# One row of w, one more transpose by DMA, products moved to GpSimd, and a new order for 889 tasks

## The chip, the cores and the metric

The kernel runs on one core of a Trainium2 chip. That core has five engines with queues of their own: TensorE (PE in the profile; its weight loads are PEld), VectorE (DVE), ScalarE (ACT), GpSimd (POOL) and SyncE (SP), and 16 DMA engines that all queues share. The metric is the device time of one execution in microseconds (us); lower is better. The kernel before takes 161.94 us (median of three runs, 161.53 to 162.7).

## The reference

Two layers follow each other. The first is a linear attention with a decaying state, for 4 batches, 8 heads, 768 steps and 48 channels a head:

```python
for t in range(S):
    kt, vt, rt = (k[:, :, t], v[:, :, t], r[:, :, t])
    cur = np.einsum('bhd,bhe->bhde', u[None] * kt, vt)
    y[:, :, t] = np.einsum('bhd,bhde->bhe', rt, state + cur)
    state = w[None, :, :, None] * state + np.einsum('bhd,bhe->bhde', kt, vt)
```

Its output, with the heads side by side, is x (4 batches of 768 x 384). The second is an MLP mixer, first over the tokens, then over the channels:

```python
xt = x.transpose(0, 2, 1)
h = np.maximum(xt @ w_tok1, 0.0) @ w_tok2
u = x + h.transpose(0, 2, 1)
h2 = np.maximum(u @ w_ch1, 0.0) @ w_ch2
return u + h2
```

w_tok1 is 768 x 256, w_ch1 is 384 x 1536. All inputs and the output are float32; the kernel multiplies in bfloat16.

## The kernel before, in words

**Tiling.** Batches are numbered b=0 to 3 in the code. A batch has six chunks of 128 steps. Within a chunk the attention is done with matrices: k and r are scaled by powers of w (tables that ScalarE makes once, as the exponential of ln w times a position), turned so that the channels lie on the partitions, and multiplied into scores (`sc`, tile at_ps). A mask cuts the scores (tile AT, on VectorE), and `y` takes AT times v plus r times the state S of the chunks before. What a step adds with its own k and v (the part with the vector u of the input) is a sum over r, k and u (tile adg) times v (`own`, tiles yd and ydb). The result is x_b, in bfloat16.

b=0 takes its chunks in three pairs (`pair_unit`): one load brings two chunks, the four scaled products of a pair (`scaled`, k and r, two each) multiply two operands in SBUF, PE turns them, and wide copies of 1024 columns (`evac_k`, `evac_r`) bring them out of PSUM. b=1 turns by PE as well; b=2 and b=3 turn k and r by a DMA transpose from SP's queue (`turn_rk`).

**Mixer.** Each batch has: `hid` (tile h_ps, with w_tok1, then a relu to h1r), `back` (with w_tok2), the channel layer `up` (tile z_ps: 24 tasks of three matmuls a batch, twelve for each half `sg` of the tokens), a relu to zr on ScalarE or VectorE, and `down` (tile h_ps, three steps of four products for each of six token blocks), then a sum or copy to osb and a store.

The layer `up` needs u = x + h turned. There are two ways, chosen by the list `DIRECT` for each (batch, half):

- direct: PE turns x (`turn_x`, nine matmuls of 128 columns), adds the backward product on top in the turned form (`back_T`), and three copies out of PSUM give uT. u itself is never made in its plain form; so the last `down` step of each block adds it with three more matmuls of 128 columns (tile h_ps from ident and uT), and the output is a copy.
- not direct: `back` gives h in the plain form, three sums on VectorE make u (`sum_u`, tile u_sb), one DMA transpose on SP's queue makes uT (`turn_dma`), and the output is a sum of u and the `down` product on VectorE.

**Order.** Everything is a task. `ORDER` lists all task numbers, written out by hand; the kernel emits its instructions in that order, so it is the program order of every engine and queue. `ENGINES` says, for each task that can go either way, which of its two engines takes it (for a product of two SBUF operands 0 is GpSimd and 1 VectorE). `BUFS` gives the buffer number of each tile, and with it what a task must wait for before it can overwrite. Twenty tasks of PE (`keep_warm`, tile kv_ps from warm) are matmuls of 512 columns without a use, put between the first real ones.

**Start.** w is read as two rows of 192, to partitions 0 and 64 (`read_w`, lines 355 to 359). Each row is spread to 128 partitions by a matmul with ones (`spread_w`, lines 447 to 451), ScalarE takes ln of each half (line 454), and the tables follow (`decay`, line 467). The weights are read by DMAs from GpSimd's queue (`load_weights`, line 581): the two token weights first, then two parts of w_ch1, then three of w_ch2. In that queue they stand between GpSimd's products.

```python
DIRECT = [(0, 0), (0, 1), (1, 0)]
PRODUCT = {"POOL": "mul2_POOL", "DVE": "mul2_DVE"}
w_rows = [wp[z * P:z * P + 1, 0, 0:dm // 2] for z in range(2)]
```

Nearly all instructions carry line 274 in the profile, which is the helper that records every operation; they are told apart by their tiles.

Of the kernel before, what the change touches and what calls it, by code (L numbers as in the profile page):

```python
# [11 lines left out]
f32 = mybir.dt.float32  # L12
# [54 lines left out]
    0, 1, 2, 0, 1, 0, 2, 0, 1, 2, 0, 1, 2, 1, 0, 1, 2, 1, 0, 2, 1, 0, 2, 1,  # L67
    ],
    'AT1': [
    0, 1, 2, 0, 1, 0, 2, 0, 1, 2, 0, 2, 1, 0, 2, 1, 0, 2, 1, 0, 2, 0, 1, 2,  # L70
# [11 lines left out]
    0, 1, 2, 3, 4, 0, 1, 2, 3, 0, 4, 3, 1, 2, 3, 0, 4, 2,  # L82
# [11 lines left out]
    0, 1, 2, 3, 4, 5, 0, 2, 1, 5, 3, 4, 0, 3, 2, 1, 0, 5, 3, 4, 2, 1, 5, 3, 0, 4, 2,  # L94
# [3 lines left out]
    0, 1, 2, 3, 4, 5, 0, 1, 2, 4, 3, 5, 4, 1, 2, 3, 5, 0,  # L98
# [16 lines left out]
    ],  # L115
    'osb': [
    0, 1, 2, 0, 2, 2, 0, 2, 0, 1, 0, 0, 2, 1, 0, 1, 0, 1, 1, 0, 2, 0, 1, 2, 0,
# [8 lines left out]
    0, 1, 2, 3, 0, 1, 2, 3, 0, 1, 2, 3,  # L126
# [9 lines left out]
    0, 1, 1, 0, 1, 0, 1, 0, 1, 0, 0, 1,  # L136
    ],
    'rt': [
    0, 1, 2, 3, 4, 2, 0, 1, 3, 2, 4, 0,
# [3 lines left out]
    0, 1, 2, 3, 0, 1, 2, 3,  # L143
    ],
    'u_sb': [
    0, 1, 2, 1, 2, 0, 1, 2,
    ],
    'vb': [
    0, 1, 2, 3, 4, 0, 1, 2, 3, 0, 4, 1, 2, 0, 3, 1, 4, 0,
    ],  # L150
    'vt': [
    0, 1, 2, 3, 4, 5, 1, 0, 2, 3, 4, 1, 5, 0, 2, 3, 4, 1,
# [5 lines left out]
    0, 1, 2, 0, 1, 2, 0, 1, 2, 0, 1, 2, 2, 1, 0, 2, 1, 0,  # L158
# [5 lines left out]
    0, 1, 2, 0, 1, 2, 0, 1, 2, 0, 1,  # L164
    ],
}
ENGINES = [
# [21 lines left out]
    0, 1, 2, 3, 4, 5,  # L189
]  # L190
H1_PARTS = [[(0, 1), (2, 3), (4, 5)], [(0, 1, 2, 3, 4, 5)], [(0, 1, 2, 3, 4, 5)], [(0, 1, 2, 3, 4, 5)]]
DIRECT = [(0, 0), (0, 1), (1, 0)]
PART = 4
STORE = ['SP', 'SP', 'SP', 'SP']

# [40 lines left out]
def kernel(  # L236
# [73 lines left out]
    def row(src):  # L310
        return src.rearrange("h d -> (h d)")
# [930 lines left out]
```

## Time and profile before

| | |
|---|---|
| median of three runs | 161.94 us |
| the profiled execution | 161.46 us |
| its span, first to last instruction | 159.8 us |
| TensorE busy | 154.1 us, 1584 matmuls |
| VectorE busy | 116.2 us, 231 instructions |
| ScalarE busy | 74.0 us, 167 |
| GpSimd busy | 71.1 us, 96 |
| DMA | 26.31 MB, 165 GB/s in the mean |
| granted TensorE clock | 0.998 |

The page gives the busy time of each engine, the span in 40 slices of 4 us with the busy share in tenths, and the chain that ended last: from the last instruction back, at each step to what released it. A line of a group reads: engine, operation, output tile <- input tiles, shapes, count | busy us in all, ns of one | idle time of the engine before them, and who ended it. A line of the chain or of a timeline begins with its start and its length in us. For a DMA issue the time is the issue's; the landing has a line of its own.

### The profile page before, as it was taken

How to read it: one execution, taken by the hardware profiler on the slowest of the kernel's cores; microseconds unless marked ns; L12 is line 12 of the kernel's file. 1: busy time of each engine (PE TensorE's matmuls, PEld its weight loads, DVE VectorE, ACT ScalarE, POOL GpSimd, SP SyncE). 2: the span in 40 equal slices, each digit the busy share in tenths (PEclk: the TensorE clock that was granted, in tenths of full speed). 3: DMA queues.
4: the chain of work that ended last, by engine and by line, in shares of the span. 5: the costliest groups of instructions: out<-in, count | busy, mean ns of one | idle time of the engine just before them, and what ended most of it. 6: DMA issues, size and time to landing. Idle time of an engine off the chain costs nothing.

```text
span 159.8 us, 3993 instructions
## 1 busy us (share of the span) xinstructions
PE 154.1 (96%) x1584; PEld 103.5 (65%) x1584; DVE 116.2 (73%) x231; ACT 74.0 (46%) x167; POOL 71.1 (45%) x96
## 2 busy tenths in 40 slices
PE   6999899999999899999999999999999999999992
PEld 2475676767776576667667766677666656666662
DVE  6499997777987589879999839978988363620422
ACT  3784685649977432264722541167431202365000
POOL 7599872392970403559163465419854000000000
PEclk9999999999999999999999999999999999999999
DMA  4999999989799797869999998998990146040052
GB/s 125 264 242 216 187 228 211 206 176 230 125 226 219 136 219 174 181 120 174 213 196 225 247 228 101 220 240 178 151 181 4 49 102 146 8 144 0 3 194 98
DMA packets 86824, 26.31 MB, mean 165 GB/s; under 512 B 81555, under 2 KB 85910, under 8 KB 86806
## 3 DMA queue, kind: packets, MB, share of 16 engines
q1 hardware_dynamic: 81328, 22.22, 68.5%
q0 software_dynamic: 5280, 3.74, 15.5%
q8 instruction: 12, 0.20, 0.5%
q10 hardware_dynamic: 198, 0.11, 0.2%
q14 instruction: 6, 0.05, 0.1%
HBM read 20.46 MB, written 4.72 MB: 158 GB/s over the span
## 4 chain that ended last, share of the span: by engine, by line
PE 84%; DVE 5%; DMA 5%; POOL 1%; issue 1%; ACT 1%; DVEq 0%; ACTq 0%
PE h_ps L274 33%; PE z_ps L274 27%; PE kv_ps L274 6%; DMA wch<-in_moe_w_ch_dram 5%; PE y_ps L274 5%; PE at_ps L274 3%; PE hT_ps L274 3%; PE hx_ps L274 3%; DVE kr L274 2%; PE tr_ps L274 2%; DVE AT L274 1%; PE w_ps L274 1%; POOL kr L274 1%; ACT S L274 1%; DVE zr L274 1%
## 5 line engine op out<-in xcount | busy, mean ns | idle before, releaser
L274 PE MATMUL h_ps<-wch,zr 128*128 128x384 bf16 (+1 forms) x300 | 52.7, 319 | 0.4 <-DMA wch<-in_moe_w_ch_dram 0.4
L274 PE MATMUL z_ps<-uT,wch 128*128 128x384 bf16 x288 | 52.1, 327 | 0.0
L274 ACT ACTIVATE zr<-z_ps 128x384 bf16<-128x384 f32 x62 | 28.2, 494 | 27.9 <-PE z_ps L274 27.2
L274 PEld LDWEIGHTS <-wch 128*128 128x128 bf16 x288 | 30.9, 114 | 12.5 <-DMA uT<-u_sb 0.2
L274 PEld LDWEIGHTS <-zr 128*128 128x128 bf16 x300 | 27.9, 98 | 16.7 <-issue 0.7
L274 DVE TENSOR_SCALAR zr<-z_ps 128x384 bf16<-128x384 f32 x34 | 18.1, 552 | 11.4 <-PE z_ps L274 11.2
L274 DVE TENSOR_TENSOR AT<-at_ps,mask 128x512 bf16<-128x512 f32 x36 | 22.9, 680 | 2.3 <-PE at_ps L274 2.3
L274 POOL TENSOR_TENSOR yd<-vb,adg 128x384 f32<-128x384 bf16 x15 | 12.3, 831 | 25.6 <-ACT vb L274 14.5
L274 DVE TENSOR_TENSOR osb<-u_sb,h_ps 128x384 f32<-128x384 bf16 (+1 forms) x16 | 8.4, 526 | 14.1 <-PE h_ps L274 13.7
L274 PEld LDWEIGHTS <-kr 128*128 128x128 bf16 (+1 forms) x196 | 12.6, 98 | 4.8 <-issue 1.3
L274 ACT CAST S<-kv_ps 48x192 bf16<-48x192 f32 (+1 forms) x26 | 9.1, 351 | 13.9 <-PE kv_ps L274 9.7
L274 POOL TENSOR_TENSOR kr<-rt,wp 128x384 bf16<-128x384 f32 x8 | 9.7, 1221 | 10.6 <-ACT wp L274 8.3
L274 POOL TENSOR_TENSOR kr<-kt,wnat 128x384 bf16<-128x384 f32 x8 | 8.4, 1053 | 7.3 <-ACT wnat L274 3.9
L274 DVE TENSOR_TENSOR x_b<-y_ps,yd 128x384 bf16<-128x384 f32 x18 | 9.8, 551 | 2.6 <-PE y_ps L274 2.2
L274 PEld LDWEIGHTS <-wtok 128*128 128x128 bf16 x78 | 7.3, 98 | 4.5 <-DVE x_b L274 0.2
L274 ACT CAST vb<-vt 128x384 bf16<-128x384 f32 x18 | 9.0, 514 | 2.4 <-DMA vt<-in_v_dram 2.4
L274 PE MATMUL kv_ps<-warm 128*128 128x512 bf16 x20 | 7.6, 505 | 1.4 <-DVE warm L274 1.4
L274 PE MATMUL h_ps<-x_b,wtok 128*128 128x384 bf16 x48 | 8.6, 326 | 0.0
L274 DVE TENSOR_TENSOR u_sb<-x_b,hT_ps 128x384 bf16<-128x384 bf16 x15 | 7.7, 549 | 1.3 <-PE hT_ps L274 1.2
L274 POOL TENSOR_TENSOR ku<-kt,u_bc 128x384 f32<-128x384 f32 x8 | 8.0, 1003 | 1.3 <-DVE rku L274 1.3
L274 DVE TENSOR_TENSOR AT<-at_ps,u_sb 128x512 bf16<-128x512 f32 x12 | 7.9, 680 | 0.3 <-PE at_ps L274 0.2
L274 ACT ACTIVATE h1r<-h_ps 128x384 bf16<-128x384 f32 x5 | 2.3, 490 | 10.4 <-PE h_ps L274 10.4
(104 smaller groups left out, 207.8 us busy)
## 6 DMA issues: line engine op xcount, KB each, us to landing
out_dram<-osb SPq DMA_DIRECT2D x23, 192.0 KB, 2.0
kt<-in_k_dram SPq DMA_DIRECT2D x18, 192.0 KB, 6.0
vt<-in_v_dram SPq DMA_DIRECT2D x18, 192.0 KB, 4.4
rt<-in_r_dram SPq DMA_DIRECT2D x12, 192.0 KB, 3.7
wch<-in_moe_w_ch_dram POOLq DMA_DIRECT2D x4, 384.0 KB, 6.3
zr<-in_r_dram SPq DMA_DIRECT2D x3, 384.0 KB, 4.8
zr<-in_k_dram SPq DMA_DIRECT2D x3, 384.0 KB, 5.5
win<-in_r_dram SPq DMA_DIRECT2D x3, 384.0 KB, 8.1
```

The costliest lines, as they stand in the source:

```text
L274: return lambda *args, **kw: tc.keep_in_program_order(f(*args, **kw))
```

## The change

Four things.

1. w is read as one row of 384 with one DMA, spread by one matmul and taken through one ln.
2. `DIRECT` loses (1, 0): the first half of u of b=1 (the second batch) goes the way that is not direct. So PE's `turn_x` and `back_T` of it become `back`, three copies become three sums on VectorE, one DMA transpose joins SP's queue, the last `down` steps of that half lose their three matmuls, and its three outputs become sums on VectorE.
3. `ENGINES` is anew. Of the twelve scaled products of b=0, GpSimd has four (all of the third pair) and VectorE eight; before it was two and ten. Other choices differ too: of the products of k, r and u of b=2, GpSimd has 17 of 24 and VectorE 7, before 10 and 14.
4. `ORDER` and `BUFS` are anew: 889 tasks instead of 894.

```diff
 ORDER = [
-    2, 26, 14, 19, 25, 0, 886, 24, 59, 10, 63, 62, 884, 9, 878, 888, 3, 16, 4, 1, 5, 22, 28, 60, 66, 29, 6,
...
+    21, 57, 3, 0, 22, 18, 24, 19, 11, 1, 58, 56, 16, 25, 2, 59, 8, 869, 62, 887, 6, 4, 13, 5, 60, 883, 63,
...
 ]
 BUFS = {
...
     'u_sb': [
-    0, 1, 2, 1, 2, 0, 1, 2,
+    0, 1, 2, 1, 2, 0, 2, 1, 0,
     ],
...
 }
 ENGINES = [
-    0, 1, 1, 1, 1, 1, 1, 1, 1, 0, 1, 1, 0, 0, 0, 0, 0, 0, 0, 0, 1, 1, 0, 1, 1, 0, 0, 0, 0, 0, 0, 1, 0, 0, 0,
...
+    1, 0, 0, 1, 0, 0, 1, 1, 1, 0, 1, 1, 1, 1, 0, 0, 0, 1, 1, 0, 1, 1, 0, 1, 1, 0, 1, 0, 0, 0, 0, 1, 0, 0, 0,
...
 ]
-DIRECT = [(0, 0), (0, 1), (1, 0)]
+DIRECT = [(0, 0), (0, 1)]
...
-    ones = const.tile([P + 1, 128], f32, name="ones")
+    ones = const.tile([1, 128], f32, name="ones")
...
-    w_rows = [wp[z * P:z * P + 1, 0, 0:dm // 2] for z in range(2)]
+    w_row = wp[0:1, 0, :]
...
-    def read_w(z):
-        return lambda: act.dma_start(w_rows[z], row(w)[z * dm // 2:(z + 1) * dm // 2].unsqueeze(0))
-
-    t_wrow0 = once("ACT", "dma_tiny", read_w(0))
-    t_wrow = once("ACT", "dma_tiny_b", read_w(1), [t_wrow0])
+    t_wrow = once("ACT", "dma_tiny", lambda: act.dma_start(w_row, row(w).unsqueeze(0)))
...
-            pe.matmul(U[key], ones[0:1, :], src, start=True, stop=True)
+            pe.matmul(U[key], ones, src, start=True, stop=True)
...
-    t_wbc = [once("PE", f"spread_{z}", spread_w(z), [(t_wrow0, t_wrow)[z], t_ones], take=("m",)) for z in range(2)]
-    t_lnw = [once("ACT", "act192", ln_w(z), [t_wbc[z], t_tab], use=[(t_wbc[z], "m")]) for z in range(2)]
+    t_wbc = once("PE", "spread", spread("w", w_row), [t_wrow, t_ones], take=("m",))
+    t_lnw = once("ACT", "act384", lambda: act.activation(lnw, U["w"], Ln), [t_wbc, t_tab], use=[(t_wbc, "m")])
...
```

More of the change, by code (lines that the diff above doesn't have):

```diff
@@ L66 @@
     'AT0': [
-    0, 1, 2, 0, 1, 0, 2, 0, 1, 2, 0, 1, 2, 1, 0, 1, 2, 1, 0, 2, 1, 0, 2, 1,
+    0, 1, 2, 0, 2, 0, 1, 0, 2, 1, 0, 1, 2, 0, 1, 2, 0, 1, 2, 0, 1, 2, 0, 2,
     ],
     'AT1': [
-    0, 1, 2, 0, 1, 0, 2, 0, 1, 2, 0, 2, 1, 0, 2, 1, 0, 2, 1, 0, 2, 0, 1, 2,
+    0, 1, 2, 0, 2, 0, 1, 0, 2, 1, 0, 2, 1, 0, 2, 1, 0, 2, 1, 0, 2, 1, 0, 2,
     ],
@@ L81 @@
     'adg': [
-    0, 1, 2, 3, 4, 0, 1, 2, 3, 0, 4, 3, 1, 2, 3, 0, 4, 2,
+    0, 1, 2, 3, 4, 1, 0, 3, 2, 4, 1, 0, 2, 3, 1, 4, 0, 1,
     ],
@@ L93 @@
     'kp': [
-    0, 1, 2, 3, 4, 5, 0, 2, 1, 5, 3, 4, 0, 3, 2, 1, 0, 5, 3, 4, 2, 1, 5, 3, 0, 4, 2,
+    0, 1, 2, 3, 4, 5, 2, 3, 5, 0, 1, 4, 3, 2, 5, 0, 1, 2, 5, 4, 3, 0, 2, 1, 4, 3, 5,
     ],
@@ L97 @@
     'kt': [
-    0, 1, 2, 3, 4, 5, 0, 1, 2, 4, 3, 5, 4, 1, 2, 3, 5, 0,
+    0, 1, 2, 3, 4, 5, 0, 1, 3, 2, 4, 5, 0, 1, 3, 4, 2, 5,
     ],
@@ L106 @@
     'm': [
[8 rows of a table removed]
[8 rows of a table added]
     ],
     'osb': [
-    0, 1, 2, 0, 2, 2, 0, 2, 0, 1, 0, 0, 2, 1, 0, 1, 0, 1, 1, 0, 2, 0, 1, 2, 0,
+    0, 1, 2, 0, 0, 2, 0, 2, 1, 0, 2, 0, 1, 1, 2, 1, 0, 2, 0, 1, 2, 0, 1, 2, 0,
     ],
@@ L125 @@
     'rk': [
-    0, 1, 2, 3, 0, 1, 2, 3, 0, 1, 2, 3,
+    0, 1, 2, 3, 0, 1, 2, 3, 1, 0, 2, 3,
     ],
@@ L135 @@
     'rku': [
-    0, 1, 1, 0, 1, 0, 1, 0, 1, 0, 0, 1,
+    0, 1, 0, 1, 0, 1, 0, 1, 0, 0, 1, 0,
     ],
     'rt': [
-    0, 1, 2, 3, 4, 2, 0, 1, 3, 2, 4, 0,
+    0, 1, 2, 3, 4, 0, 2, 1, 4, 0, 3, 1,
     ],
@@ L142 @@
     'uT': [
-    0, 1, 2, 3, 0, 1, 2, 3,
+    0, 1, 2, 3, 1, 0, 2, 3,
     ],
     'u_sb': [
-    0, 1, 2, 1, 2, 0, 1, 2,
+    0, 1, 2, 1, 2, 0, 2, 1, 0,
     ],
     'vb': [
-    0, 1, 2, 3, 4, 0, 1, 2, 3, 0, 4, 1, 2, 0, 3, 1, 4, 0,
+    0, 1, 2, 3, 4, 1, 0, 3, 2, 4, 1, 0, 3, 2, 4, 1, 0, 2,
     ],
     'vt': [
-    0, 1, 2, 3, 4, 5, 1, 0, 2, 3, 4, 1, 5, 0, 2, 3, 4, 1,
+    0, 1, 2, 3, 4, 5, 1, 0, 2, 3, 4, 5, 1, 2, 0, 3, 4, 5,
     ],
@@ L157 @@
     'yd': [
-    0, 1, 2, 0, 1, 2, 0, 1, 2, 0, 1, 2, 2, 1, 0, 2, 1, 0,
+    0, 1, 2, 1, 0, 2, 1, 0, 2, 1, 0, 2, 0, 1, 2, 1, 0, 2,
     ],
@@ L163 @@
     'zr': [
-    0, 1, 2, 0, 1, 2, 0, 1, 2, 0, 1,
+    0, 1, 2, 2, 0, 1, 0, 2, 1, 0, 2,
     ],
@@ L443, in f @@
             U[key] = ps(f"{key}_ps", [128, dm])
-            pe.matmul(U[key], ones[0:1, :], src, start=True, stop=True)
+            pe.matmul(U[key], ones, src, start=True, stop=True)
         return f
-    def spread_w(z):
-        def f():
-            U["w", z] = ps(f"w{z}_ps", [128, dm // 2])
-            pe.matmul(U["w", z], ones[z * P:z * P + 1, :], w_rows[z], start=True, stop=True)
-        return f
-    def ln_w(z):
-        return lambda: act.activation(lnw[:, z * dm // 2:(z + 1) * dm // 2], U["w", z], Ln)
-    t_wbc = [once("PE", f"spread_{z}", spread_w(z), [(t_wrow0, t_wrow)[z], t_ones], take=("m",)) for z in range(2)]
-    t_lnw = [once("ACT", "act192", ln_w(z), [t_wbc[z], t_tab], use=[(t_wbc[z], "m")]) for z in range(2)]
+    t_wbc = once("PE", "spread", spread("w", w_row), [t_wrow, t_ones], take=("m",))
+    t_lnw = once("ACT", "act384", lambda: act.activation(lnw, U["w"], Ln), [t_wbc, t_tab], use=[(t_wbc, "m")])
     t_wd = once("PE", "tiny_mm", cast_wd, [t_wh, t_idf], take=("m",))
@@ L468, in decay @@
         return once("ACT", "act384s", lambda: act.activation(t[:, g, :], lnw, Exp, scale=iota[:, col:col + 1]),
-                    t_lnw + deps)
+                    [t_lnw] + deps)
     t_wp2 = [decay(wp2, j, 2 + j, [t_io2]) for j in range(2)]
     t_wk2 = [once("ACT", "act384s", lambda j=j: act.activation(early["wk", j], lnw, Exp, scale=iota[:, j:j + 1]),
-                  t_lnw + [t_io2, t_ewk[j]], use=use_wk[j]) for j in range(2)]
+                  [t_lnw, t_io2, t_ewk[j]], use=use_wk[j]) for j in range(2)]
     t_wn = {G: [decay(wn[G], g, (4 if G == 2 else 6) + g, [t_io]) for g in range(G)] for G in USED}
@@ L510 @@
     wps = {3: wp}
-    t_wp = {3: [decay(wp, g, 6 + NG + g, [t_io, t_us, t_wd, t_ud, t_uw] + t_wbc) for g in range(NG)]}
+    t_wp = {3: [decay(wp, g, 6 + NG + g, [t_io, t_wbc, t_us, t_wd, t_ud, t_uw]) for g in range(NG)]}
     if 2 in TABLES:
```

114 rows, old and new, of tables (BUFS, ENGINES, ORDER) are left out of this document.

## The prediction

> **What bounds the kernel now.** I read the busy table first, then the slices of the DMA engines, then the chain of work that ended last, and after that the queues of the engines the change touches.
>
> ```profile
> span 159.8 us, 3993 instructions
> PE 154.1 (96%) x1584; PEld 103.5 (65%) x1584; DVE 116.2 (73%) x231; ACT 74.0 (46%) x167; POOL 71.1 (45%) x96
> DMA  4999999989799797869999998998990146040052
> ```
>
> TensorE (PE) is busy 154.1 of 159.8 us; no other engine comes near. The DMA engines stand at eight or nine tenths in nearly every slice up to the thirtieth (120 us), so they are the second bound: loads must be asked for early, and little is left for more.
>
> The chain in order of time shows where PE was not the one that counted:
>
> ```profile
> 1.39 1.89 PE kv_ps L274 x4
> 3.28 1.59 PE w_ps L274 x4
> ...
> 15.26 2.66 DVE kr L274 x2
> ...
> 28.41 2.30 PE hx_ps L274 x22
> ...
> 44.44 8.20 DMA wch<-in_moe_w_ch_dram
> ...
> 62.72 0.17 PE hx_ps L274 x3
> ...
> 100.62 0.55 PE at_ps L274 x16
> ...
> 105.09 3.90 PE z_ps L274 x24
> ...
> 156.85 0.36 DVE osb L274
> ```
>
> ```profile
> PE h_ps L274 <- DMA wch<-in_moe_w_ch_dram: 0.4, 1, 0.4
> ```
>
> PE works from 1.39 to about 156.85. Of its 5.7 us without work (159.8 - 154.1), 1.39 lie before and 2.95 (159.8 - 156.85) behind, so 1.4 us are all that any new order could still fill. The rest of the chain that is not PE is two VectorE (DVE) products at 15.26, and one weight load that landed at 52.64 (44.44 + 8.20) and for which, by the table of waits, PE stood 0.4 us. A matmul of 384 columns costs 3.90/24 = 162.5 ns, one of 128 columns 0.17/3 = 57 ns; so four of the first take 0.65.
>
> **Time outside the span.** The profiled execution took 161.46 for a span of 159.8, so 1.66 lie around it; the median 161.94 is 0.48 above that execution. I work in the span and add 2.14.
>
> **First u of b=1 by DMA.** Removed from PE: nine turns of x and nine additions of u in the last down steps, all of 128 columns. The `back` products stay six of 384 columns, only with the operands exchanged. PE saves 18 x 57 ns = 1.0 us, on the path, since PE is full there.
>
> ```profile
> L274 ACT CAST uT<-hx_ps 128x384 bf16<-128x384 f32 x5 | 2.3, 482 | 3.7 <-PE hx_ps L274 3.7
> L274 DVE TENSOR_TENSOR u_sb<-x_b,hT_ps 128x384 bf16<-128x384 bf16 x15 | 7.7, 549 | 1.3 <-PE hT_ps L274 1.2
> L274 SPq DMA_TRANSPOSE uT<-u_sb x5: 1249/1292/2010, 68.1 to 132.8; - x5
> DMA to landing us min/median/max: 4.0/4.0/4.0
> ```
>
> Instead of a 0.48 us copy, the first `up` now waits for a DVE sum and a DMA that lands 4.0 us after SyncE (SP) starts to issue it. The u's three chunks leave PE 2 x 162.5 = 325 ns apart and a sum takes 549, so the last sum ends 0.55 + 2 x 0.22 = 1.0 after the last product: 5.0 us to the landing. What covers it: behind the last of these products the new list has seven PE tasks before the first `up`: three `down` (0.65), three `down` that end in a residual (0.65 + 0.17 = 0.82) and one score of two chunks (0.55), 4.96 us. No slack, and just ahead in SP's queue stands the turn of a k and r of b=2, another transpose, whose issue takes as long as this one's, 1.29. I take 0.4 us of new waiting; the ends are 0 and 1.3, more if loads block SP (first rival). The three DVE sums (1.65 us) replace two copies on ACT and one on DVE; of the three outputs of this u, two go from ACT to DVE (1.1). DVE's idle time, below, covers both.
>
> **w as one row.** One DMA, one spread (two passes) and one Ln instead of two each.
>
> ```profile
> 4.91 0.33 ACT L274 ACTIVATE lnw<-w_ps 128x192 f32<-128x192 f32 x1 [0.33 <-PE w_ps L274]
> 5.27 1.12 ACT L274 ACTIVATE wpair<-lnw,iota 128x384 f32<-128x384 f32 x2
> ```
>
> Now the second half of Ln ends at 5.24 (4.91 + 0.33) and the decays start. One spread of 384 columns streams what the two streamed; bounds are half of the 1.59 and the whole. From the same start, 3.28, it ends between 4.1 and 4.9, and an Ln of twice the width (estimate 0.5) between 4.7 and 5.4. I take no change: gain 0.6, loss 0.2 at the ends. The u row's spread moves up next to it, in place of fill-in matmuls, whose number stays 20.
>
> **The first 25 us.** Here the DVE decides.
>
> ```profile
> 5.92 1.06 DVE L274 TENSOR_TENSOR kr<-zr,wpair 128x384 bf16<-128x384 f32 x2 [0.77 <-ACT wpair L274]
> 19.50 2.47 DVE L274 TENSOR_TENSOR AT<-at_ps,u_sb 128x512 bf16<-128x512 f32 x4
> 24.16 0.68 DVE L274 TENSOR_TENSOR AT<-at_ps,u_sb 128x512 bf16<-128x512 f32 x1
> L274 DVE TENSOR_TENSOR pr<-tr_ps,ka 128x1024 bf16<-128x1024 bf16 x3 | 2.1, 685 | 0.2 <-ACT ka L274 0.2
> L274 ACT COPY rkb<-tr_ps 128x1024 bf16<-128x1024 bf16 x6 | 6.1, 1013 | 0.9 <-PE tr_ps L274 0.6 <-DVE pr L274 0.2
> ```
>
> From its first product to the last mask of the third pair it needs 5.92 to 24.84, 18.9 us. The new list puts there: eight products (0.53 each, 4.2) instead of ten, a wide copy of r that ACT did (1.1, estimate from ACT's 1.01), three k-r products (2.1), twelve masks (0.62, 7.4), five sums or copies of 384 columns (0.55, 2.8), three copies of sums, two memsets and u_blk (about 1.1): 18.7. So moving two products to GpSimd (POOL) frees what the other moves fill: zero, with -1.1 and +1.0 as ends. What they add to POOL matters more. In its queue the second token weight now stands behind four scaled products, one table, four `own` products and a k product of b=1.
>
> ```profile
> 12.50 1.96 POOL L274 TENSOR_TENSOR kr<-zr,u_sb 128x384 bf16<-128x384 f32 x2
> 14.40 1.44 POOL L274 DMA_DIRECT2D wtok<-in_moe_w_tok_dram  x2
> 15.86 1.63 POOL L274 TENSOR_TENSOR ydb<-zr,adg 128x384 bf16<-128x384 bf16 x2
> DMA to landing us min/median/max: 8.4/9.2/9.9
> ```
>
> That last line is the two token weights'. The issue of the second and third pair's k follows, then the landing of the pair loads and of the five channel weights.
>
> ```profile
> 3.17 2.77 SPq L274 DMA_DIRECT2D zr<-in_k_dram  x2
> DMA to landing us min/median/max: 3.8/6.1/8.7
> DMA to landing us min/median/max: 5.4/6.6/9.6
> ```
>
> Before, both were issued by 15.84, and the second was in by about 25 (14.40 + 0.72 + 9.9). After: the third pair's k is in by about 10.7 (issued about 3.17 + 2.77/2 = 4.6, landing as the pair loads' median, 6.1); then 5 products of 0.98, the first token weight's issue (0.7), and five of 0.82 make 20.4. Landing 8.4 to 9.9 gives 28.8 to 30.3. Its first use is the backward product that stands in the piece at 28.41 of the chain. Wait 0.4 to 1.9; with the channel weights' 6.6 it is none. I take 0.2, near the latter, since the DMA that slowed the token weights is the pair loads', which are over by then.
>
> **The other moves.** On POOL 47 products instead of 37, 19 `own` instead of 20; DVE tasks 228 to 241, ACT 162 to 141. Thirteen tasks more, at most 0.55 us each, are 7 us of DVE's 43 idle ones: no bound. The last weight, which PE waited 0.4 us for at 52.64, now has 8.9 us of PE work between issue and use in the list, against 6.2: that wait goes, -0.4; the one next to it has 6.5 against 7.1. The rest of the list I cannot price wait by wait. It can gain at most the remaining 1 us of PE's idle time and lose more; with DMA that full I take +0.4. The tail keeps its half products and 2.95 us; the half that ends last is now stored over ACT, 0 (ends -0.3, +0.3).
>
> **Sum.** 156.85 - 1.0 - 0.4 + 0.4 + 0.2 + 0.4 = 156.45; + 2.95 = 159.4 of span; + 2.14 = 161.5 us.
>
> **Rivals.**
>
> *SP's queue holds up the new transpose (slower).*
>
> ```profile
> L274 SPq DMA_DIRECT2D kt<-in_k_dram x18: 368/1284/4368, 8.9 to 104.4; - x18
> ```
>
> [...] If the transpose ahead and such a load are still to be issued when the sums are done, the first `up` waits 1.29 + 1.28 = 2.6 to 1.29 + 4.37 = 5.7 us, against 0.4 in my sum: 163.7 to 166.8, the lower end likelier. It decides once the issue starts more than 1 us after the last sum. For it: the DMA slices. Against: all five transposes of u so far landed in 4.0 us.
>
> *The start becomes shorter (faster).* The two products in the chain at 15.26 took 2.66 where the first two took 1.06. Without that excess of 1.6, and if half of the wide copy's 1.1 falls into waits, the start shortens by 1.1; and all weights come in time. 161.5 - 1.1 - 0.2 - 0.4 - 0.4 = 159.4.
>
> *Products on POOL hold up DVE.*
>
> ```profile
> L274 DVE TENSOR_TENSOR kr<-zr,wpair x6: 552/598/2172, 5.9 to 15.7; 128x384 bf16<-128x384 f32 x6
> ```
>
> The one that took 2172 instead of 552 ns started at 15.7, beside two POOL products in a row (15.86 to 17.49). Ten more POOL products give ten more such places; one that PE must wait for costs 1.6 us: 163.1. Against: this one is now on POOL itself, and DVE then has masks, which read PSUM. The Trainium skill, GPSIMD Engine Reference, Key points, says that GpSimd shares its SBUF interfaces with VectorE and contends with VectorE instructions that have two SBUF inputs. By that rule every such meeting is to be counted; the trace agrees in this one place, while its median of 598 says that most pass unharmed.
>
> **Chances.** My forecast 0.41 (160.4 to 162.6), SP's queue 0.26, the shorter start 0.23, POOL against DVE 0.10. One per cent, about what a measurement of this kernel can tell from no change, is 160.3 and 163.6. Faster: the third case, 0.23 and a little of the first; slower: most of the second and some of the last, 0.25. Low end 159.4, the faster case; high end 164.2, half a us above the likelier end of SP's.
>
> **What would show it.** Right: matmuls of h_ps from ident and uT 18 instead of 27, and as many of hx_ps from ident; six uT transposes; PE busy about 153; the last mask of the third pair near 25; no wait for wch over 0.3. Wrong: PE or its weight loads waiting for uT or wtok by more than 1 us, a mask of the third pair after 26 or before 24, DVE products over 2 us with PE idle behind them, or PE idle for more than 3 us in all inside its stretch.

## The result, and the profile after

The changed kernel took 163.93 us (median of four executions, 163.07 to 164.63), the kernel before 161.74 in four beside them (161.44 to 162.7): a ratio of 1.0121, with a 95% interval of 1.0071 to 1.0170. By that it is slower by 1.2%. Two of the four executions had a mean granted clock of 0.989 and 0.990 and took 164.19 and 164.63; the other two had 1.0 and took 163.07 and 163.66. The experiments measured the same kernel twice more, in more executions, at 1.0021 (0.9976 to 1.0065) and 1.0044 (0.9995 to 1.0092): some of the 1.2% did not come back, and both of these intervals hold 1, so the later executions do not show the change to be slower. All ratios here leave out executions more than 1.5% above the fastest of their kernel (in the third measurement seven of twelve) and the medians leave out none; by the medians the three ratios are 1.0135, 1.0031 and 1.0077.

The profile is of the execution with 164.19 us. From its page, the span, the busy table and the granted clock by slices:

```profile
span 162.5 us, 3939 instructions
PE 154.7 (95%) x1562; PEld 103.2 (64%) x1564; DVE 121.8 (75%) x244; ACT 67.1 (41%) x147; POOL 78.7 (48%) x102
PE   6999999999999999994999999899999999999992
PEclk9999999999999999998799999999999999999999
```

TensorE (PE) has 20 weight loads fewer (1564 against 1584: 18 by the change of `DIRECT` and two by the one spread of w; of its matmuls two records are missing) and is no less busy. One slice, the nineteenth (73 to 77 us), is only four tenths full, and the clock falls in that slice and the next. The waits name who kept PE:

```profile
PE z_ps L274 <- DVE zr L274: 2.3, 2, 2.1
PE z_ps L274 <- DMA uT<-u_sb: 0.5, 1, 0.5
```

One wait of 2.1 us, for a relu on VectorE (DVE) that frees a PSUM bank. The timelines at that place (start, length, engine, output <- inputs), first VectorE's and PE's, then GpSimd's (POOL):

```profile
25.05 0.35 DVE L274 CAST vb<-vt 128x384 bf16<-128x384 f32 x1
...
69.93 1.16 DVE L274 CAST vb<-vt 128x384 bf16<-128x384 f32 x1
71.01 2.63 DVE L274 TENSOR_TENSOR kr<-kt,wnat 128x384 bf16<-128x384 f32 x2
73.57 1.14 DVE L274 CAST vb<-vt 128x384 bf16<-128x384 f32 x1
74.64 1.47 DVE L274 TENSOR_SCALAR zr<-z_ps 128x384 bf16<-128x384 f32 x3
...
72.77 0.34 PE L274 MATMUL kv_ps<-vb,kr 128*128 128x96 bf16 x4
75.23 4.28 PE L274 MATMUL z_ps<-uT,wch 128*128 128x384 bf16 x15 [2.13 <-DVE zr L274]
```

```profile
69.73 1.14 POOL L274 TENSOR_TENSOR ku<-kt,u_bc 128x384 f32<-128x384 f32 x1 [2.52 <-DMA kt<-in_k_dram]
70.84 1.12 POOL L274 TENSOR_TENSOR kr<-rt,wp 128x384 bf16<-128x384 f32 x1
71.92 1.31 POOL L274 TENSOR_TENSOR rku<-ku,rt 128x384 f32<-128x384 f32 x1
73.19 1.30 POOL L274 TENSOR_TENSOR kr<-rt,wp 128x384 bf16<-128x384 f32 x1
```

A cast that takes 0.35 us at 25.05, with no product on GpSimd, takes 1.16 at 69.93; two k products take 2.63, where each takes 0.55 alone. Both engines go in step: the first GpSimd product ends at 70.87 (69.73 + 1.14) and the cast at 71.09, the second at 71.96 and the first k product after it, and so on, one VectorE instruction for one GpSimd product. Cast, two products and cast take 4.8 us (69.93 to 74.71), alone 0.35 + 2 x 0.55 + 0.35 = 1.8. The relus behind them come 3.0 us late; 0.9 of that must have been slack, since PE stood for 2.13. Then its 15 matmuls take 4.28 us; in two experiments below the same 15 take 2.60, so 1.7 are lost to the clock. Together 3.8 us in one place.

### The profile page after: what moved, and what is told of

The parts are those of the page before. It is cut to its first block, busy times and chain, and to the rows that moved or that the text cites. A ratio compares the mean times of both kernels' runs of the same rounds, so it can differ in the third digit from the quotient of the medians.

```text
span 162.5 us, 3939 instructions
## 1 busy us (share of the span) xinstructions
PE 154.7 (95%) x1562; PEld 103.2 (64%) x1564; DVE 121.8 (75%) x244; ACT 67.1 (41%) x147; POOL 78.7 (48%) x102
## 4 chain that ended last, share of the span: by engine, by line
PE 76%; DVE 11%; DMA 7%; issue 2%; ACT 1%; SPq 1%; DVEq 0%
PE h_ps L274 31%; PE z_ps L274 25%; PE y_ps L274 5%; DMA zr<-in_r_dram 4%; PE at_ps L274 3%; PE hT_ps L274 3%; PE kv_ps L274 3%; DMA uT<-u_sb 3%; PE hx_ps L274 2%; DVE kr L274 2%; DVE AT L274 2%; DVE yd L274 2%; DVE vb L274 1%; SPq L274 1%; PE tr_ps L274 1%
## 5 line engine op out<-in xcount | busy, mean ns | idle before, releaser
L274 PE MATMUL z_ps<-uT,wch 128*128 128x384 bf16 x288 | 54.2, 334 | 2.8 <-DVE zr L274 2.3
L274 ACT ACTIVATE zr<-z_ps 128x384 bf16<-128x384 f32 x59 | 27.4, 492 | 49.8 <-PE z_ps L274 49.7
L274 DVE TENSOR_SCALAR zr<-z_ps 128x384 bf16<-128x384 f32 x37 | 19.2, 551 | 6.7 <-PE z_ps L274 6.6
L274 POOL TENSOR_TENSOR rku<-ku,rt 128x384 f32<-128x384 f32 x10 | 10.3, 1032 | 16.3 <-DVE adg L274 8.5
L274 DVE TENSOR_TENSOR osb<-u_sb,h_ps 128x384 f32<-128x384 bf16 (+1 forms) x19 | 9.8, 528 | 7.7 <-PE h_ps L274 7.5
L274 ACT CAST S<-kv_ps 48x192 bf16<-48x192 f32 (+1 forms) x24 | 8.2, 340 | 14.9 <-PE kv_ps L274 8.4
L274 POOL TENSOR_TENSOR kr<-rt,wp 128x384 bf16<-128x384 f32 x10 | 10.7, 1070 | 7.0 <-DMA rt<-in_r_dram 7.0
L274 POOL TENSOR_TENSOR kr<-kt,wnat 128x384 bf16<-128x384 f32 x11 | 11.3, 1029 | 4.8 <-PE z_ps L274 4.1
L274 DVE TENSOR_TENSOR u_sb<-x_b,hT_ps 128x384 bf16<-128x384 bf16 x18 | 9.1, 550 | 3.8 <-PE hT_ps L274 3.8
L274 ACT CAST vb<-vt 128x384 bf16<-128x384 f32 x12 | 6.1, 513 | 3.5 <-DMA vt<-in_v_dram 3.4
```

Source lines behind the costliest of these rows:

```text
L274: return lambda *args, **kw: tc.keep_in_program_order(f(*args, **kw))
```

## The experiments

**Theory:** products on GpSimd, run back to back in b=2, hold up VectorE's products of two SBUF operands and its casts from SBUF; PE waits for what is queued behind, and the idle time brings the clock down. **Rivals:** VectorE simply has too much to do there; the new transpose, SP's queue or the loads are the cause; or the first comparison was a matter of the clock. All kernels are the changed one with the edit shown, and each stands against executions of the kernel before taken beside it (medians there 162.51, 162.13 and 161.93 us).

### Fewer products on GpSimd

In `ENGINES`, 0 and 1 are GpSimd and VectorE for a product, ScalarE and VectorE for a cast or relu.

```diff
-    1, 0, 0, 0, 1, 1, 0, 0, 0, 0, 1, 1, 1, 1, 0, 0, 0, 0, 1, 0, 0, 0, 0, 0, 0, 1, 0, 0, 0, 1, 0, 0, 0, 0, 0,
+    1, 0, 0, 0, 1, 1, 0, 1, 1, 0, 1, 1, 1, 1, 1, 0, 0, 0, 1, 0, 0, 0, 0, 0, 0, 1, 0, 0, 0, 1, 0, 0, 0, 0, 0,
```

> Three products of b=2 (k times u of the fifth chunk, r times its table and k r u of the fourth) go from GpSimd back to VectorE, in the same places of the list. VectorE gets 3 x 0.55 = 1.65 us more to do between 68 and 80 us, GpSimd 3 us less. If products on GpSimd hold up VectorE (theory): its casts to vb there take 0.35 us instead of 1.1 and its k products 0.55 instead of 1.36, TensorE's wait of 2.13 us for a relu goes (under 0.3), the clock stays at 1.00, and the time is 160.2 to 161.2 us. If VectorE simply has too much to do in that stretch (rival): the wait grows by the 0.55 us of the product that stands ahead of the relu, to about 2.7, and the time is 164.5 to 165.5. If the new transpose or the loads are the cause: 163.9 as before.

160.62 us, ratio 0.9943 (0.9893 to 0.9992). The trace is of the longest of its ten executions, 163.91 us. VectorE's timeline there, with three products more than in the changed kernel:

```profile
70.16 0.55 DVE L274 TENSOR_TENSOR ku<-kt,u_bc 128x384 f32<-128x384 f32 x1
70.63 0.35 DVE L274 CAST vb<-vt 128x384 bf16<-128x384 f32 x1
70.89 1.65 DVE L274 TENSOR_TENSOR kr<-kt,wnat 128x384 bf16<-128x384 f32 x2
72.47 0.35 DVE L274 CAST vb<-vt 128x384 bf16<-128x384 f32 x1
72.74 1.01 DVE L274 TENSOR_SCALAR zr<-z_ps 128x384 bf16<-128x384 f32 x2
73.67 1.38 DVE L274 TENSOR_TENSOR kr<-rt,wp 128x384 bf16<-128x384 f32 x1
```

With more to do, VectorE is through earlier: casts 0.35, products 0.55 where GpSimd stands idle. That rules out "too much to do". The wait is 0.61 us and not under 0.3: two meetings are left (1.1 of the 1.65, and the 1.38), the last with a product that GpSimd now did later.

The clock did not stay at 1.00 in this trace, for a reason elsewhere: in b=3 four products of VectorE now stood beside GpSimd's and took 4.2 us (109.12 to 113.33) where they took 2.2 in the first trace (112.61 to 114.77). PE waited 0.67, 0.16 and 0.25 us for the sums and outputs behind them, and from 115.99 to 119.40 us it ran at half speed. One meeting less in b=2, and in this execution one more in b=3.

### The relus that PE waits for, on ScalarE

```diff
-    0, 1, 1, 0, 0, 0, 0, 1, 0, 0, 1, 0, 1, 0, 0, 0, 0, 1, 1, 0, 0, 0, 0, 0, 1, 1, 1, 0, 1, 0, 0, 0, 1, 0, 0,
-    0, 0, 0, 0, 1, 0, 0, 0, 1, 1, 0, 0, 1, 0, 0, 0, 0, 0, 1, 0, 0, 0, 0, 0, 0, 1, 0, 0, 1, 1, 1, 0, 0, 0, 1,
+    0, 1, 1, 0, 0, 0, 0, 1, 0, 0, 1, 0, 1, 0, 0, 0, 0, 1, 1, 0, 0, 0, 0, 0, 1, 1, 1, 0, 1, 0, 0, 0, 0, 0, 0,
+    0, 0, 0, 0, 1, 0, 0, 0, 1, 0, 0, 0, 0, 0, 0, 0, 0, 0, 1, 0, 0, 0, 0, 0, 0, 1, 0, 0, 1, 1, 1, 0, 0, 0, 1,
```

> Three relus of b=1, which VectorE does at 74.6 to 76.1 us behind its slow casts and products, go to ScalarE, which stood idle there from 73.5 to 76.9; GpSimd's products stay. If a late relu is all that TensorE waited for (theory, and the rival that VectorE has too much to do): VectorE's casts and products are as slow as before (1.1 and 1.36 us), the wait of 2.13 us and the fall of the clock go all the same, 160.5 to 161.5 us. If TensorE would have had to wait there in any case (for uT, a weight or a buffer): a wait of 1 to 2 us stays under another name, 163 to 164.

161.78 us, ratio 0.9936 (0.9877 to 0.9995). The timelines of VectorE and PE:

```profile
71.37 1.16 DVE L274 CAST vb<-vt 128x384 bf16<-128x384 f32 x1
72.45 2.63 DVE L274 TENSOR_TENSOR kr<-kt,wnat 128x384 bf16<-128x384 f32 x2
75.00 1.16 DVE L274 CAST vb<-vt 128x384 bf16<-128x384 f32 x1
...
74.21 0.33 PE L274 MATMUL kv_ps<-vb,kr 128*128 128x96 bf16 x4
74.38 2.60 PE L274 MATMUL z_ps<-uT,wch 128*128 128x384 bf16 x15
```

VectorE is as slow as before, to two hundredths, and PE does not wait there. So uT, weights and buffers were there, and the late relu was all. Another wait of the same kind shows in this trace: at 41.34 us PE has stood 1.41 us for a relu behind a cast of VectorE that took 1.47 beside a product of GpSimd. In the three traces of the changed kernel this wait is 0, 0.18 and 0.35. The median lies 0.3 us above the range; the kernel before, too, stood higher beside it (162.51) than in the first comparison (161.74).

### The casts on ScalarE

```diff
-    0, 0, 0, 0, 1, 0, 0, 0, 1, 1, 0, 0, 1, 0, 0, 0, 0, 0, 1, 0, 0, 0, 0, 0, 0, 1, 0, 0, 1, 1, 1, 0, 0, 0, 1,
-    1, 0, 0, 0, 1, 1, 0, 0, 0, 0, 1, 1, 1, 1, 0, 0, 0, 0, 1, 0, 0, 0, 0, 0, 0, 1, 0, 0, 0, 1, 0, 0, 0, 0, 0,
+    0, 0, 0, 0, 1, 0, 0, 0, 1, 1, 0, 0, 1, 0, 0, 0, 0, 0, 1, 0, 0, 0, 0, 0, 0, 1, 0, 0, 1, 1, 1, 0, 0, 0, 0,
+    1, 0, 0, 0, 1, 0, 0, 0, 0, 0, 1, 1, 1, 0, 0, 0, 0, 0, 1, 0, 0, 0, 0, 0, 0, 1, 0, 0, 0, 1, 0, 0, 0, 0, 0,
```

> Three casts to vb of b=2, which VectorE does at 69.9, 73.6 and 76.5 us, go to ScalarE; GpSimd's products stay. If products on GpSimd hold up VectorE (theory): the two k products stay at 1.36 us each, the relu comes 1.16 + 1.14 = 2.3 us earlier, the wait goes to under 0.3 us and the time to 160.3 to 161.5. If only the amount of VectorE's work counts (rival): a cast is worth what it takes by itself, 0.35 us, so 0.7 less ahead of the relu, a wait of 1.4 us, 162.7 to 163.5.

162.12 us, ratio 0.9954 (0.9898 to 1.0010), an interval that holds 1: it is the trace that tells here, again that of the longest execution (164.08). The same timelines:

```profile
70.72 2.63 DVE L274 TENSOR_TENSOR kr<-kt,wnat 128x384 bf16<-128x384 f32 x2
73.28 1.47 DVE L274 TENSOR_SCALAR zr<-z_ps 128x384 bf16<-128x384 f32 x3
...
72.47 1.62 PE L274 MATMUL z_ps<-uT,wch 128*128 128x384 bf16 x9 [0.21 <-ACT zr L274]
```

The k products stay at 2.63 beside GpSimd's, and taking the casts away removes the whole wait for VectorE, not 0.7 us of it: a cast there was worth its slowed length. The median is 0.6 us above the range; the trace has a fall of the clock, at another place (0.57 granted from 116 to 120 us), behind the same waits in b=3 as in the first run's trace (0.68, 0.16 and 0.25).

### Two more products given to GpSimd in b=3

```diff
-    1, 0, 0, 0, 1, 1, 0, 0, 0, 0, 1, 1, 1, 1, 0, 0, 0, 0, 1, 0, 0, 0, 0, 0, 0, 1, 0, 0, 0, 1, 0, 0, 0, 0, 0,
-    0, 0, 1, 0, 1, 0, 0, 0, 0, 1, 1, 0, 0, 0, 0, 0, 0, 0, 0, 1, 0, 1, 0, 0, 1, 0, 0, 1, 1, 0, 0, 0, 0, 0, 0,
+    1, 0, 0, 0, 1, 1, 0, 1, 1, 0, 1, 1, 1, 1, 1, 0, 0, 0, 1, 0, 0, 0, 0, 0, 0, 1, 0, 0, 0, 1, 0, 0, 0, 0, 0,
+    0, 0, 1, 0, 1, 0, 0, 0, 0, 1, 1, 0, 0, 0, 0, 0, 0, 0, 0, 1, 0, 0, 0, 0, 1, 0, 0, 0, 1, 0, 0, 0, 0, 0, 0,
```

> As the run that gives three products of b=2 back to VectorE, and besides the two own products of b=3 that VectorE did at 108.6 and 109.5 us (0.97 and 1.35) go to GpSimd, in line behind its r products there. By the theory the wait of 0.21 us at 111 goes too: 160.0 to 161.0 us. By the rival (amount of VectorE's work): 164.3 to 165.3.

163.69 us, ratio 1.0076 (1.0018 to 1.0134): a miss, on the other side. The wait at 111 went, and a larger one came behind it, in the timelines of VectorE and PE:

```profile
108.30 2.54 DVE L274 TENSOR_TENSOR ku<-kt,u_bc 128x384 f32<-128x384 f32 x2
110.76 1.36 DVE L274 TENSOR_TENSOR kr<-rt,wp 128x384 bf16<-128x384 f32 x1
112.04 1.34 DVE L274 TENSOR_TENSOR kr<-kt,wnat 128x384 bf16<-128x384 f32 x1
...
114.00 0.21 PE L274 MATMUL at_ps<-rk 48*128 48x128 bf16 x1 [1.56 <-DVE x_b L274]
```

With the own products behind it in the queue, GpSimd was still at work when VectorE's next four products came: 5.1 us (108.30 to 113.38) instead of 4 x 0.55 = 2.2, and the sums to x_b, whose PSUM banks the next scores need, stood behind them. Though not meant so, this is a second case of the theory: the same mechanism, another place and another victim. The rival doesn't explain it, since VectorE had two products less than in the first run. But this wait is only 0.9 us longer than in the first run's trace (0.67), and the two ratios lie 1.3% apart, 2.2 us: what made the rest stays open.

### The changed kernel and the kernel before, again

No edit.

> The changed kernel once more, unaltered, to see what of its loss is the same in every execution. In the traces so far the granted clock changes on a grid of 3.413 us whose place differs from run to run: full speed begins at 8.6 to 10.9 us, and a grid step with much idle time of TensorE is followed by one at half speed. If the 163.9 us are the change's own (theory: products on GpSimd that hold up VectorE, then the clock): 163 to 164.5 us again, casts and products of VectorE beside GpSimd's at 1.1 to 1.36 us between 69 and 76 us, and a wait of TensorE for a relu there of 1 to 2.2 us. If the place of the grid in a few runs made it (rival): a median of 161.5 to 162.5, and the same waits with or without a fall of the clock.

162.63 us, ratio 1.0021 (0.9976 to 1.0065).

> The kernel before once more, unaltered, for a second trace. If the grid of the clock moves freely: full speed begins at another time than the 8.83 us of the first trace, anywhere in a stretch of 3.4 us, and for each us that it begins later the first product of the channel layer (31.2 us) starts up to 0.5 us later. If the start of TensorE's work sets the grid: 8.8 again, within 0.1.

One execution, 161.23 us. The trace records full speed from 9.11 us, the first trace from 8.83: beyond the 0.1 of a fixed start, but one near pair is little (the first `z_ps` starts at 31.04 instead of 31.19). The changed kernel's traces settle it. Their PE timelines are the same up to 8.04 us, and full speed is recorded from 10.92 in the first and 8.22 in the second, so the start of TensorE's work does not set the grid. The second trace also says what comes back. PE's timeline has the wait to the hundredth, and no fall of the clock behind it:

```profile
74.96 2.27 PE L274 MATMUL z_ps<-uT,wch 128*128 128x384 bf16 x13 [2.13 <-DVE zr L274]
```

So the wait belongs to the change; the 1.7 us behind it do not come every time. The median lies a tenth above the rival's range, and below the theory's: beside these ten, the first four executions overstated the loss.

> The changed kernel a third time, unaltered, in more executions and beside the two below. The second time it stood at 1.0021 of the kernel before, not at the first time's 1.0121, with the same wait of 2.13 us and no fall of the clock. If the loss is the wait alone and the fall of the clock is a matter of where the grid stands (theory): 162.3 to 163.3 us, 1.002 to 1.007 of the kernel before. If the first comparison was right: 1.010 or more.

163.18 us, ratio 1.0044 (0.9995 to 1.0092), 160.65 to 165.34 in twelve executions. The trace is of the fastest, and in its timelines of VectorE and PE the wait is short:

```profile
69.83 0.35 DVE L274 CAST vb<-vt 128x384 bf16<-128x384 f32 x1
70.09 1.83 DVE L274 TENSOR_TENSOR kr<-kt,wnat 128x384 bf16<-128x384 f32 x2
71.85 1.15 DVE L274 CAST vb<-vt 128x384 bf16<-128x384 f32 x1
...
73.52 2.60 PE L274 MATMUL z_ps<-uT,wch 128*128 128x384 bf16 x15 [0.52 <-DVE zr L274]
```

GpSimd's first product started at 70.08 here, 0.35 us later than in the first trace, and found VectorE already at work: the first cast and one of the k products passed unharmed, and 1.6 of the 2.1 us were gone. How large the wait is hangs on who comes first.

### The relus once more

No edit beside the three relus.

> The changed kernel with three relus of b=1 on ScalarE, a second time. If the wait of 2.13 us behind VectorE's slow products is what the changed kernel loses (theory): 1.3 to 2.1 us below the run of the unaltered changed kernel beside it, 160.5 to 161.3, and 0.990 to 0.996 of the kernel before. If that wait only shifts and is paid later (rival): within 0.6 us of the unaltered one.

161.16 us, ratio 0.9938 (0.9894 to 0.9981). Beside the unaltered changed kernel it is 1.7 us faster by the two ratios and 2.0 by the two medians (163.18), and the intervals of the ratios do not touch. The wait is not paid back later.

### The first half of u of b=1 direct again

On top of the run with fewer products on GpSimd:

```diff
-DIRECT = [(0, 0), (0, 1)]
+DIRECT = [(0, 0), (0, 1), (1, 0)]
```

`ORDER` keeps its places: `turn_x` and `back_T` stand where `back` stood, the copies where the sums stood; `ENGINES` and `BUFS` get the entries that the copies need.

> The run with three products given back to VectorE, and besides the first half of u of b=1 direct again, as in the kernel before: 18 matmuls of 128 columns more on TensorE, three sums and one DMA transpose less, all else in its place. If the new transpose saves what the prediction said (18 x 57 ns = 1.0 us on TensorE, with no wait for uT): TensorE's busy time is 0.9 to 1.1 us longer at the same clock, and the time 0.6 to 1.2 us above that run, 161.2 to 161.8. If the transpose, the sums or SP's queue cost something: the time is equal or lower, 160 to 160.6.

162.88 us, ratio 1.0010 (0.9963 to 1.0058), against 0.9943 for its base: 0.7%, 1.1 us, the size expected, though the median lies 1.1 us above its range. PE's busy time, 154.4 us, is 1.2 above the base's 154.9 without the 1.7 lost to the clock there. But the intervals overlap, the two were measured at different times, and this trace has a wait of 1.22 us at 41.40 for the relu behind the cast, 0.16 in the base's. So this supports the saving of 1.0 us and does not prove it.

### Three attempts at a faster order

The first two stand on the run with fewer products on GpSimd and turn VectorE's list at 105 to 115 us, the second further. This is the first's edit there; two casts went to ScalarE as well, and the cast at 39 us behind two relus:

```diff
-    653, 632, 732, 744, 710, 641, 663, 616, 752, 721, 755, 726, 654, 742, 747, 705, 655, 733, 711, 642, 756,
+    653, 632, 732, 705, 744, 710, 711, 641, 642, 663, 616, 752, 721, 755, 726, 654, 742, 747, 655, 733, 756,
```

> The run with three products given back to VectorE, and besides two casts of b=2 on ScalarE, and VectorE's list turned in two places so that no relu and no sum that TensorE waits for stands behind a product of two SBUF operands (the cast at 39 us behind two relus; two x_b sums and a relu of b=3 ahead of four products at 108 to 113 us). If products beside GpSimd's are what makes those late (theory): TensorE's waits at 40, 75 and 112 to 115 us (0.16, 0.61 and 1.25 in that run) go to under 0.2 each, no fall of the clock inside, 159.5 to 160.5 us, 1% under the kernel before. If VectorE has too much to do as a whole (rival): the waits move to the next relu or sum, 160.6 or more.

162.83 us, ratio 1.0043 (1.0001 to 1.0085): a miss. The x_b sums and the relu went ahead; now two outputs stood behind the same products, with banks that the same scores need, in PE's timeline:

```profile
115.13 0.38 PE L203 MATMUL at_ps<-rk 48*128 48x128 bf16 x7 [1.08 <-DVE osb L203]
```

The second puts these outputs ahead, too:

> The run in which VectorE's list was turned in two places, turned further: at 105 to 115 us two relus and two sums of outputs, too, stand ahead of the products of two SBUF operands, and the two products that the next transposes wait for are the first of them; the second token weight is asked for earlier, the cast at 39 us stands later. By the theory TensorE's waits at 22 (0.59), 40 (0.46), 107 (0.24) and 114 us (1.08 in that run) go, and 160.0 to 161.0 us come out, 0.986 to 0.995. If VectorE as a whole is too full: new waits for masks or for rk of 0.5 us and more, 161.5 and up.

162.84 us, ratio 1.0034 (1.0002 to 1.0065): a miss, as its rival said. The wait is now one for a mask, at 118.90, 1.08 us, and it is of another kind: the mask stood behind a sum that waited 0.90 us for a product of GpSimd, which came late because the two products of VectorE that it needs had been put last (115.78; they took 1.02, unharmed). So turning the list moved the wait and did not shorten it, and these two runs do not tell the theory from its rival for that stretch. The third is the three relus on ScalarE with two moves, and leaves that stretch alone:

```diff
-    356, 347, 243, 248, 380, 357, 239, 267, 348, 349, 83, 358, 123, 257, 80, 350, 272, 340, 246, 247, 249,
+    356, 243, 248, 380, 357, 239, 267, 348, 349, 83, 358, 123, 257, 80, 350, 347, 272, 340, 246, 247, 249,
...
-    145, 146, 167, 136, 71, 140, 188, 163, 137, 190, 147, 138, 150, 191, 148, 164, 165, 74, 149, 189, 151,
+    145, 146, 167, 136, 71, 140, 188, 163, 137, 190, 147, 138, 120, 150, 191, 148, 164, 165, 74, 149, 189, 151,
```

(347 is the cast, 120 the second token weight, which is taken out of its old place.)

> As the run with three relus on ScalarE, and besides the second token weight is asked for 2.6 us of GpSimd's products earlier, and one cast of b=1 at 39 us stands behind the two products of r, k and u that it held up. If the waits of TensorE for the weight (0.2 to 1.0 us where the clock rises early) and at 40 us (0 to 1.4) are real: both under 0.1, 160.0 to 160.8 us, 0.987 to 0.994 of the kernel before. If they are paid back elsewhere: as that run, 160.5 to 161.3.

161.29 us, ratio 0.9928 (0.9889 to 0.9966): faster than both kernels, by 0.7% against the one before; the ratio is as expected, the median half a us above its range. No wait for the weight is left in its trace; at 41.5 us PE waits 0.43 for the cast that was moved. Against the three relus alone (0.9938) the two moves show no gain that can be told.

## Why the prediction was right or wrong

The forecast was 161.5 us and no change; 163.93 lies outside that, inside the range of 159.4 to 164.2. The two later medians, 162.63 and 163.18, lie within the 160.3 to 163.6 that the prediction called no change, so the size of the first miss was in part chance. The wait was not: it is in all three traces of the changed kernel (2.13, 2.13 and 0.52 us), and the prediction had it nowhere in its sum. In the span of the first trace: 159.4, with the 0.4 for "the rest of the new order" replaced by the wait of 2.13, is 161.1; with the clock's 1.7 it is 162.8; measured are 162.5, so all other terms together came out 0.3 us better than priced.

**The 18 matmuls: right.** The instructions on the tile h_ps in the first trace have the count that was announced:

```profile
L274 PE MATMUL h_ps<-ident,uT x18: 218/219/220, 54.3 to 67.3; 128*128 128x128 bf16 x18
```

and the list of DMA issues has six transposes of uT (count, us to the landing):

```profile
uT<-u_sb SPq DMA_TRANSPOSE x6, 3.9
```

PE's busy time holds the clock's losses, so two traces without a fall inside compare best, the second of the kernel before and the third of the changed one, by the busy tables of their pages:

```profile
PE 153.7 (96%) x1583; PEld 103.5 (65%) x1584; DVE 116.5 (73%) x231; ACT 73.9 (46%) x167; POOL 71.1 (45%) x96
```

```profile
PE 152.5 (96%) x1562; PEld 102.1 (64%) x1564; DVE 120.4 (76%) x244; ACT 66.9 (42%) x147; POOL 78.9 (50%) x102
```

1.2 us less, against 1.0. In the first trace 154.7 less the 1.7 lost to the clock is 153.0, as announced.

**The new transpose (+0.4) and SP's queue: none.** The first `z_ps` of b=1 started at 67.41 without a wait, and none came there in the other two traces. The 0.5 us for uT in the waits above is b=2's; the second trace of the kernel before has the same wait, 0.45 us at 100.93.

**The weight w_ch2 (-0.4) and the start (0): right by their signs.** No wait for wch is left; but the second trace of the kernel before has none either, so the 0.4 was a matter of one execution and not of the kernel. The last masks of the third pair ended at 24.67 (23.39 + 1.28), "near 25", in VectorE's timeline of the first trace:

```profile
23.39 1.28 DVE L274 TENSOR_TENSOR AT<-at_ps,u_sb 128x512 bf16<-128x512 f32 x2
```

The first `z_ps` came somewhat later, at 31.83, 31.35 and 31.33 in the three traces against 31.19 and 31.04.

**The second token weight (+0.2): right in size.** No wait in the first trace, 0.45 and 0.21 us in the others, and up to 1.03 in an edited kernel (the first run with three relus on ScalarE).

**The step that failed** is "thirteen tasks more, at most 0.55 us each, are 7 us of DVE's 43 idle ones: no bound", and with it the 0.4 for the rest. It took a share of idle time over the whole span where one stretch of 5 us decided, and at most 0.55 us a task, where products and casts take 1.1 to 1.36 beside GpSimd's. What the runs showed in its place is the wait of 2.13 us. The move to GpSimd lightened VectorE by ten products, seven of them in b=2; what counted is that the rest stood beside a row of GpSimd products, ahead of relus.

**The rival that came true** was the third, at 0.10. Its mechanism was right, its price near (1.6 us for 2.13), its place wrong: it looked at the first 25 us, where the row stood, and found masks there. The argument "its median of 598 says that most pass unharmed" took products for harmless meetings that had met nobody: the other five of that row had no long GpSimd product beside them. The rule of the Trainium skill, GPSIMD Engine Reference, Key points, by which every meeting counts, was the better guide.

**The clock** was in no term. It explains why one wait cost 3.8 us in one execution and 2.1 in another.

## What to carry to other kernels

Before a product of two SBUF operands, or a cast from SBUF, is moved between GpSimd and VectorE, lay both queues side by side for that stretch: where both have such work, price VectorE at one instruction per GpSimd product, and look for what is queued behind it that frees a PSUM bank. Two cures worked, to about the same size: three products less on GpSimd in that stretch (0.9943), or TensorE's relus out of VectorE's queue, to an engine that stood idle (0.9936 and 0.9938). Turning VectorE's list around the products, on top of the first cure, did not (1.0043 and 1.0034). And where TensorE waits 2 us within 3.4, count a clock fall as possible, and compare kernels by ten executions rather than four.

## What the hardware showed

**One engine at a time.** The lock goes both ways. In the timelines of the kernel before, VectorE was first, and GpSimd stood:

```profile
62.32 0.54 DVE L274 TENSOR_TENSOR kr<-rt,wp 128x384 bf16<-128x384 f32 x1
62.79 0.55 DVE L274 TENSOR_TENSOR rku<-ku,rt 128x384 f32<-128x384 f32 x1
63.26 0.55 DVE L274 TENSOR_TENSOR kr<-rt,wp 128x384 bf16<-128x384 f32 x1
63.73 0.55 DVE L274 TENSOR_TENSOR kr<-kt,wnat 128x384 bf16<-128x384 f32 x1
...
62.42 3.67 POOL L274 TENSOR_TENSOR kr<-rt,wp 128x384 bf16<-128x384 f32 x2 [8.27 <-ACT wp L274]
```

Four products of VectorE at full speed, and two of GpSimd in 3.67 us, where two took 1.96 at 12.50. They did not take turns here: GpSimd stood until VectorE's row was over. The Trainium skill, SBUF — State Buffer, section "SBUF: two separate sides", calls the pair of ports that the two share an exclusive lock, held for the whole instruction; the traces agree. Not expected was that a cast with a single operand in SBUF is held as well (0.35 to 1.16 us); relus, masks and sums that read PSUM were not, in any trace (three relus in 1.47 us at 74.64, beside a product on GpSimd; the longest single ones in all fourteen traces are 0.56 for a relu or a sum and 0.69 for a mask).

**The clock falls by steps.** Windows of the changed kernel's first and second trace (length; then for PE, PEld, DVE, ACT and POOL the busy time and count; granted clock, DMA share, GB/s):

```profile
72.00:76.00 4.00, 1.87 (x15) 1.23 (x14) 4.00 (x6) 0.49 (x1) 4.00 (x4) 0.97 1.33 225
76.00:80.00 4.00, 4.00 (x23) 2.15 (x22) 2.73 (x6) 2.13 (x5) 2.38 (x3) 0.60 0.79 164
```

```profile
72.00:76.00 4.00, 1.87 (x16) 1.32 (x14) 4.00 (x7) 0.49 (x1) 4.00 (x4) 1.00 0.96 203
76.00:80.00 4.00, 4.00 (x43) 2.94 (x42) 4.00 (x8) 3.25 (x8) 2.13 (x3) 1.00 0.93 190
```

The same idle 2.13 us; in the first 1.72 us of clock are lost (0.03 x 4 + 0.40 x 4), which is half speed for 3.4 us, in the second none. By the Trainium skill, TensorE: Matmul & The Clock Gate, section "What's actually happening", activity is judged in windows of 3413 ns that run freely. The first trace agrees: it records half speed from 75.77 to 79.19, 3.413 us, so the step before began at 72.36 and held the whole wait (73.10 to 75.23). In the second, full speed is recorded from 8.22; nineteen steps on, a border lies at 73.07, so the wait (72.83 to 74.96) was cut, but 1.89 of it lay in one window and no fall came. And in the traces of the first and the third experiment half speed followed a step in which PE stood for no more than 1.25 us, among the scores. So how much idle time brings a fall is not shown, and idle time may not be all that counts.

The start shows the same, by eight turns of 128 columns in PE's timelines of these two traces:

```profile
9.74 1.06 PE L274 MATMUL tk_ps<-ident,kr 128*128 128x128 bf16 x8
```

```profile
9.04 0.61 PE L274 MATMUL tk_ps<-ident,kr 128*128 128x128 bf16 x8
```

At 9.7 us one execution still ran at about half speed, at 9.0 the other at full. In the eleven traces of the changed kernel and its edits that record the rise, the first `z_ps` starts at 31.07 to 31.35 where full speed came by 9.3 us and at 31.83 to 32.24 where it came after 9.8; the one exception (31.84) had waited 1.03 us for a weight. That this and the falls explain the whole spread of one kernel's executions (160.83 to 164.21 in the 34 of the kernel before that stood beside the third measurement) is argued, not shown: only one execution of each run has a trace.
